# Later preparation, later decoding and a pinned TensorE order in the last plain steps of a fused attention and two-layer kernel

## The chip, the cores and the metric

The kernel runs on one core of one Trainium2 chip. The metric is the device time of one execution in microseconds (us), as the median of several runs.

## The reference, cut to what matters

```python
def reference(**kwargs):
    attn_out = _attn_ref(q, k, v)                     # (4, 8, 576, 64), two sparse masks
    x = attn_out.transpose(0, 2, 1, 3).reshape(2304, 512)
    h = x @ w_in                                      # first layer, 512 -> 2048
    x = (h - tanh(h)) @ w_out                         # 2048 -> 512
    xn = x / sqrt(mean(x * x) + 1e-6) * rms_g         # second layer
    g, val = xn @ w_gate, xn @ w_val                  # 512 -> 1536 each
    return (g / (1 + exp(-g)) * val) @ w_out2         # 1536 -> 512
```

2304 tokens run through attention, then through a first layer, then through a second layer with a gate and a value matrix.

## The kernel before

**Precision.** Weights arrive as 64-bit floats. Each block of 128 x 512 is loaded (`fetch`, L175), put together from its two 32-bit words (ScalarE `scale`, L184 and L186; VectorE `merge`, L196), and split into a high and a low part (ScalarE `high`, L203; VectorE `low`, L207). A product is then three matmuls: high by high, high by low, low by high. All matmuls go through `mm` at L150, so tiles tell them apart.

**The second layer has two forms.** The first 256 tokens go through twelve plain steps (`for f in range(FB)`, L1388). A step f does the gate and the value product of block f (`pe_gv`, 24 matmuls `ps_h<-xn,w`), the activation chain on ScalarE and VectorE (L949 to L953), and two steps later the output product of block f (`pe_o(0, f)`, 6 matmuls `ps_x<-w,p`). The other 2048 tokens go through a scheme with seven products in place of eight (`Stage`, NJ = 2 token blocks by NP = 6 pairs of weight blocks). Its products are numbered and run as 1, then 5 and 2 in the first stage, then 6, 3, 7 and 4 (`both(m, ...)`); each has a gate and a value half of 6 matmuls, `ps_pr<-xt,wt` or `ps_pr<-xt,wo` or `ps_q<-xt,wt`. The output product of plain step 11 is issued in the first stage, behind product 1 (`second()`).

**What the stages need ready.** Two helpers run beside the plain steps:

- `pg`, the generator `preps()`. While the last group of the first layer runs, it normalises the tokens; 39 of its pieces are taken there. Seven are left when the plain steps begin: `conv(m)` for m = 1, 2, 5, 6, 3, 7, 4. Each makes the token operand `xt[m]` of product m: for 5, 6, 7 and 4 a difference (VectorE, L1039), then for each a high part (ScalarE, L1058) and a low part (VectorE, L1059), all of 128 x 1024.
- `decode`, which makes weight operands for the stages on POOL. For each pair and for gate and value it has four items: load the plain weights back from memory (`load`, SP DMA `wa<-v`, L291), sums (`sums`, 4 POOL instructions, L302), and two halves (`half`, each a POOL copy L285 and a POOL subtraction L286 into `wo`). Items 0 to 7 are pair 0: its gate (0 to 3) and its value (4 to 7); the load of both stands in item 0. Product 5 needs `got[2]` (first half of the gate) and `got[3]` (first half of the value); products 3 and 7 need `got[4]` and `got[5]`.

**Order.** A compile-time scheduler orders each engine's instructions by priority, which is program order with some pieces raised (the activation chain by 400, the stage's chain by 300), over a modelled time line. From the end of the first layer the SP queue is in program order (`manual_schedule`), so its DMAs stand as written: at each step the weight loads (`st2.to`), the stores of split weights (`store.to`, L363), then the loads of `decode`; at step 8 first `pairs[0].fetch((0, 1))` (L280). `store.plain` goes out on ScalarE's queue (L344). TensorE is in program order from behind the plain steps (L1403) on; inside the plain steps the scheduler is free, and may also put matmuls of the first stage between those of the last plain steps.

**Rooms.** Split weights, fetched weights and `wo` share 20 slots (`wts`); raw weights have 3 (`rawb`); the loaded `wa`, the sums `ws` and the differences `tr` of `conv` share 4 (`tmp`). Plain steps use PSUM banks by `f % 6`; steps 10 and 11 use `ps_x`.

Of the kernel before, what the change touches and what calls it, by code (L numbers as in the profile page):

```python
# [34 lines left out]
def attn_moe_moe_kernel(  # L35
# [25 lines left out]
    B, _, NC, D = q_str.shape  # L61
    NT, DM = out.shape
    FA = w_in.shape[0]
    FB = w_gate.shape[0]
# [16 lines left out]
    def runs(s):  # L81

        r = []
        for i, (b, t) in enumerate(subs[s]):
            if r and r[-1][0] == b and r[-1][1] + r[-1][2] == t:
                r[-1][2] += 64
            else:
                r.append([b, t, 64, 64 * i])
        return r
# [36 lines left out]
    for s in range(len(subs)):  # L126
        if len(runs(s)) > 1 or s in LANES:
            _, t0, n, _ = runs(s)[0]
# [20 lines left out]
    def mm(out_, lhsT, rhs, start, stop):  # L149
        nc.tensor.matmul(out_, lhsT, rhs, start=start, stop=stop, skip_group_check=True)  # L150
# [179 lines left out]
    decode = Decode()  # L330
# [606 lines left out]
    def pe_gv(j, f):  # L937
        r, n = [], R0
        bank = (bank_h, bank_m, bank_h, bank_m, bank_x, bank_x)[f % 6]("ps_h")
        for k, kd in enumerate(("gate", "val")):  # L940
            ps = bank[:, k * n:k * n + n]
            w, x = w2[kd, f].t, xn[j]
            seq = [(a, e, c) for c in range(4) for a, e in ((0, 0), (0, 1), (1, 0))]
            for i, (a, e, c) in enumerate(seq):
                mm(ps, w[:, a, c, :], x[:, e, c, :], i == 0, i == len(seq) - 1)
            r.append(ps)
        with tc.high_priority(400):
            s = pb.tile([128, n], F32, tag="s", name="s", bufs=3)
            nc.scalar.activation(out=s, in_=r[0], func=ACTF.Silu, scale=WS)  # L949
            nc.vector.scalar_tensor_tensor(out=s, in0=r[1], scalar=WS, in1=s, op0=ALU.mult, op1=ALU.mult)  # L950
            t = pb.tile([128, 2, n], F32R, tag="p", name="p", bufs=3)
            nc.scalar.copy(out=t[:, 0], in_=s)
            nc.vector.tensor_tensor(out=t[:, 1], in0=s, in1=t[:, 0].bitcast(F32), op=ALU.subtract)  # L953
        p_of[j, f] = t

    def pe_o(j, f):
        if f == 0:
            oacc[j] = [ps_x.tile([128, 512], F32, tag="x", name="ps_x") for _ in range(R0 // 128)]
        w, p = w2["out2", f].t.rearrange("p s c f -> p s (c f)"), p_of.pop((j, f))
        for t in range(R0 // 128):  # L960
            for i, (a, e) in enumerate(((0, 0), (1, 0), (0, 1))):
                mm(
                    oacc[j][t], p[:, e, t * 128:t * 128 + 128], w[:, a, :],
                    f == 0 and i == 0, f == FB - 1 and i == 2,
                )
# [337 lines left out]
    for g, f, a, e in units:  # L1303
        if g == 0:
            st1.to(2 * (f + 4))
        elif f == 0:
            if g == 1:
                queue0.close()
                order = ctx.enter_context(ExitStack())
# [8 lines left out]
        if g == NG - 2 and f == 14:  # L1318
# [3 lines left out]
            order = ctx.enter_context(ExitStack())  # L1322
# [65 lines left out]
    for f in range(FB):  # L1388
        if f == FB - 4:
            pairs[0].fetch((0, 1))  # L1390
        st2.to(max(3 * (f + 2), N1 + (len(w2_order) - N1) * (f + 1) // (FB - 2)))
        store.plain(st2.i - 1)
        store.to(st2.i - 6)
        pe_gv(0, f)
        for _ in range(3 if f < FB - 2 else 40):
            next(pg, None)
        decode.to(max(0, min(8, 8 * (f - 4) // 6)))
        if f > 1:
            pe_o(0, f - 2)
    pe_o(0, FB - 2)  # L1400
    store.plain(len(w2_order))
    store.to(len(w2_order))
    ctx.enter_context(tc.manual_schedule(engines={mybir.EngineType.PE, mybir.EngineType.SP}))  # L1403

    def second():
# [149 lines left out]
```

## Time and profile before

| | before |
|---|---|
| median of 3 runs | 888.45 us (885.4 to 888.65) |
| profiled execution, its own time | 887.88 us |
| its span (first to last instruction) | 886.1 us |
| mean granted TensorE clock | 0.992 |
| TensorE (PE) busy | 866.5 us, 98% of the span |
| VectorE (DVE) busy | 629.8 us, 71% |
| ScalarE (ACT) busy | 413.9 us, 47% |
| POOL busy | 250.6 us, 28% |

Busy times are shares of the whole span; stages differ. "Idle before" is time in which the engine stood still just before an instruction, with what released it. A matmul's end is modelled, so the distance between two starts is the better measure of a run of matmuls.

### The profile page before, as it was taken

To read this page: it belongs to the slowest core of one execution; us is meant where nothing else is said; L and a number is where in the kernel's file an instruction comes from. 1 tells how busy PE (TensorE), PEld (TensorE's weight loads), DVE (VectorE), ACT (ScalarE), POOL (GpSimd) and SP (SyncE) were. 2 spreads that over 40 slices of the span, in tenths; PEclk is the share of its full clock that TensorE was granted. 3 is DMA by queue.
4 is the path that set the end of the run, shared out by engine and by line. 5 is a ranking of instruction groups with operands and counts; after the bars stand their busy time and mean duration, and the time that the engine had idled before them with its cause. 6 is when DMAs were issued, how large, how long until landed. Compare 5 with 4: busy or idle time off the path is not lost.

```text
span 886.1 us, 14047 instructions
## 1 busy us (share of the span) xinstructions
PE 866.5 (98%) x5091; PEld 722.7 (82%) x5091; DVE 629.8 (71%) x1290; ACT 413.9 (47%) x916; POOL 250.6 (28%) x309
## 2 busy tenths in 40 slices
PE   7999999999999999999999899999999999999998
PEld 4888888888998887888889877888788888888886
DVE  5999778888779887657778945569688553445544
ACT  6887633333543333878657644533325324322230
POOL 0000147695366853000000679846200000000000
PEclk8999999999999999999999999999999999999999
DMA  9965224311313000889977999765661288544002
GB/s 302 368 223 178 74 75 156 104 57 36 115 55 110 25 19 27 330 306 370 412 252 227 352 372 336 299 230 214 211 216 48 75 320 353 177 149 136 1 1 95
DMA packets 63717, 164.12 MB, mean 185 GB/s; under 512 B 10080, under 2 KB 21728, under 8 KB 63648
## 3 DMA queue, kind: packets, MB, share of 16 engines
q1 hardware_dynamic: 61088, 159.56, 51.1%
q10 hardware_dynamic: 2560, 3.67, 1.2%
q8 instruction: 40, 0.66, 0.3%
q14 instruction: 29, 0.24, 0.1%
HBM read 119.16 MB, written 44.04 MB: 184 GB/s over the span
## 4 chain that ended last, share of the span: by engine, by line
PE 58%; DVE 10%; POOL 7%; issue 2%; ACT 2%; DMA 1%; SPq 0%; ACTq 0%; DVEq 0%; POOLq 0%
PE ps_pr L150 20%; PE ps_o L150 14%; PE ps_h L150 10%; PE ps_x L150 9%; POOL pr L675 5%; DVE so L715 4%; PE ps_q L150 4%; POOL pr L708 1%; DVE tg L860 1%; DVE g L871 1%; DMA wt<-w 1%; DMA w<-w 1%; DVE s L1108 0%; DVE sm L451 0%; POOL ws L302 0%
## 5 line engine op out<-in xcount | busy, mean ns | idle before, releaser
L150 PE MATMUL ps_h<-xs,w 128*128 128x512 f32 (+1 forms) x984 | 214.6, 367 | 0.7 <-DVE tg L860 0.7
L150 PE MATMUL ps_x<-g,w 128*128 128x512 f32 (+1 forms) x984 | 214.2, 366 | 0.0
L150 PEld LDWEIGHTS ps_h<-xs,w 128*128 128x128 f32 x984 | 169.9, 190 | 30.5 <-DVE tg L860 1.3
L150 PEld LDWEIGHTS ps_x<-g,w 128*128 128x128 f32 x984 | 168.5, 189 | 30.4 <-ACT g L866 0.4
L150 PE MATMUL ps_pr<-xt,wt 128*128 128x512 f32 x576 | 137.6, 390 | 2.0 <-DVE s L1118 1.1
L150 PE MATMUL ps_o<-wt,p 128*128 128x512 f32 x576 | 136.0, 389 | 0.0
L150 PEld LDWEIGHTS ps_pr<-xt,wt 128*128 128x128 f32 x576 | 107.7, 188 | 26.2 <-DVE s L1118 2.0
L150 PEld LDWEIGHTS ps_o<-wt,p 128*128 128x128 f32 x576 | 108.1, 188 | 22.5
L675 POOL TENSOR_TENSOR pr<-sk,sq 128x256 f32<-128x256 f32 (+2 forms) x101 | 82.6, 852 | 133.0 <-DMA sq<-in_q_str_dram 107.3
L866 ACT CAST g<-tg 128x512 fp32r<-128x512 f32 (+1 forms) x82 | 46.5, 567 | 101.3 <-DVE tg L860 101.2
L1129 ACT COPY u<-ps_pr 128x512 f32<-128x512 f32 x72 | 41.9, 587 | 103.5 <-PE ps_pr L150 103.4
L708 POOL TENSOR_TENSOR pr<-sv,se 128x288 f32<-128x288 f32 (+12 forms) x104 | 69.7, 691 | 57.0 <-DVE so L715 19.8
L1181 DVE SCALAR_TENSOR_TENSOR osum<-ps_o,osum 128x512 f32<-128x512 f32 x80 | 54.8, 687 | 27.2 <-PE ps_o L150 26.6
L302 POOL TENSOR_TENSOR ws<-wa 128x256 f32<-128x256 f32 x24 | 24.6, 1044 | 170.4 <-DVE w L207 152.2
L715 DVE TENSOR_REDUCE so<-pr 128x16 f32<-128x272 f32 (+11 forms) x104 | 64.9, 653 | 9.0 <-POOL pr L708 8.6
L150 PE MATMUL ps_pr<-xt,wo 128*128 128x512 f32 x288 | 67.4, 389 | 0.0
L150 PEld LDWEIGHTS ps_pr<-xt,wo 128*128 128x128 f32 x288 | 54.1, 188 | 11.3
L871 DVE TENSOR_TENSOR g<-tg,g 128x512 fp32r<-128x512 f32 (+1 forms) x82 | 55.3, 676 | 10.6 <-ACT g L866 9.3
L860 DVE SCALAR_TENSOR_TENSOR tg<-ps_h,tg 128x512 f32<-128x512 f32 (+1 forms) x82 | 50.6, 618 | 15.9 <-ACT tg L855 15.6
L855 ACT ACTIVATE tg<-ps_h 128x512 f32<-128x512 f32 (+1 forms) x82 | 44.2, 540 | 34.8 <-PE ps_h L150 34.7
L196 DVE SCALAR_TENSOR_TENSOR ct<-ca,ct 128x512 uint32<-128x512 uint32 x68 | 48.0, 713 | 16.6 <-ACT ca L186 16.0
L680 DVE TENSOR_REDUCE sc<-pr 128x4 f32<-128x256 f32 (+2 forms) x101 | 43.7, 437 | 12.1 <-POOL pr L675 11.7
(121 smaller groups left out, 1045.7 us busy)
## 6 DMA issues: line engine op xcount, KB each, us to landing
wt<-w SPq DMA_DIRECT2D x84, 512.0 KB, 4.6
w<-w SPq DMA_DIRECT2D x36, 512.0 KB, 6.2
raw<-in_w_out_dram SPq DMA_DIRECT2D x28, 512.0 KB, 5.8
w<-wo SPq DMA_DIRECT2D x24, 512.0 KB, 7.4
raw<-in_w_in_dram SPq DMA_DIRECT2D x16, 512.0 KB, 8.6
raw<-in_w_gate_dram SPq DMA_DIRECT2D x12, 512.0 KB, 6.7
raw<-in_w_val_dram SPq DMA_DIRECT2D x12, 512.0 KB, 7.1
wa<-v SPq DMA_DIRECT2D x24, 256.0 KB, 4.7
```

Source lines behind the costliest of these rows:

```text
L150: nc.tensor.matmul(out_, lhsT, rhs, start=start, stop=stop, skip_group_check=True)
L196: nc.vector.scalar_tensor_tensor(out=t, in0=self.a.bitcast(U32), scalar=3, in1=t, op0=ALU.logical_shift_left, op1=ALU.bitwise_or)
L675: nc.gpsimd.tensor_tensor(out=pr, in0=self.k[:, a:e, :], in1=self.q[:, c - c0:c - c0 + 1, :].to_broadcast([128, e - a, D]), op=ALU.mult,)
L680: pend.append(lambda: nc.vector.tensor_reduce(out=s[:, c - c0, a:e], in_=pr, axis=AX.X, op=ALU.add))
L708: nc.gpsimd.tensor_tensor(out=pr, in0=self.v[:, 0:c + 1, a:e], in1=self.e[:, c - c0, 0:c + 1].unsqueeze(2).to_broadcast([128, c + 1, e - a ...
L715: pend.append(lambda: nc.vector.tensor_reduce(out=o[:, c - g0, a:e], in_=pr.rearrange("l c d -> l d c"), axis=AX.X, op=ALU.add))
L855: nc.scalar.activation(out=t, in_=h_of[g, f, a], func=ACTF.Tanh, scale=WS)
L860: nc.vector.scalar_tensor_tensor(out=t, in0=h_of.pop((g, f, a)), scalar=WS, in1=t, op0=ALU.mult, op1=ALU.subtract)
L866: nc.scalar.copy(out=t[:, 0], in_=t_of[g, f, a])
L871: nc.vector.tensor_tensor(out=t[:, 1], in0=t_of.pop((g, f, a)), in1=t[:, 0].bitcast(F32), op=ALU.subtract)
L1129: nc.scalar.copy(out=u, in_=x[kd])
L1181: nc.vector.scalar_tensor_tensor(out=o, in0=ps, scalar=WS, in1=o, op0=ALU.mult, op1=ALU.add)
```

## The change

Three things change in the loop over the plain steps, and nothing else:

- `pg` is taken later: none before step 5, two pieces at step 5, one at each of steps 6 to 9, the rest at step 10 (before: three at each of steps 0 to 9).
- `decode` is taken later: items up to 2, 4, 6 and 8 at steps 8, 9, 10 and 11 (before: up to 1, 2, 4, 5, 6 and 8 at steps 5 to 10).
- From step 10 to the end of the loop TensorE is in program order: products of step 10, output products of step 8, output products of step 9, products of step 11, output products of step 10. Behind that the order written out before goes on with product 1 of the first stage.

```diff
         store.plain(st2.i - 1)
         store.to(st2.i - 6)
+        if f == FB - 2:
+            order = ctx.enter_context(ExitStack())
+            order.enter_context(tc.manual_schedule(engines={mybir.EngineType.PE}))
+        if f == FB - 1:
+            pe_o(0, f - 2)
         pe_gv(0, f)
-        for _ in range(3 if f < FB - 2 else 40):
+        for _ in range((f >= 5) + (f == 5) if f < FB - 2 else 40):
             next(pg, None)
-        decode.to(max(0, min(8, 8 * (f - 4) // 6)))
-        if f > 1:
+        decode.to(max(0, 8 * (f - 7) // 4))
+        if 1 < f < FB - 1:
             pe_o(0, f - 2)
     pe_o(0, FB - 2)
     store.plain(len(w2_order))
     store.to(len(w2_order))
+    order.close()
     ctx.enter_context(tc.manual_schedule(engines={mybir.EngineType.PE, mybir.EngineType.SP}))
```

## Rows read from the trace of the kernel before

**Rows 1.** Busy time by stretch: plain steps, then the first stage (us, busy, instructions).

```profile
core 0: us, PE busy (x) PEld busy (x) DVE busy (x) ACT busy (x) POOL busy (x), PEclk, DMA share, GB/s
468.00:484.00 16.00, 16.00 (x118) 15.15 (x118) 15.80 (x26) 12.20 (x24) 0.00 (x0) 1.00 0.76 243
484.00:500.00 16.00, 13.45 (x76) 11.58 (x76) 16.00 (x25) 12.77 (x23) 4.57 (x2) 0.89 0.99 326
500.00:521.60 21.60, 20.17 (x123) 17.64 (x122) 14.52 (x18) 9.43 (x20) 16.40 (x15) 1.00 0.99 368
521.60:545.00 23.40, 21.90 (x95) 17.15 (x94) 14.06 (x16) 9.29 (x16) 22.79 (x26) 1.00 1.02 392
```

**Rows 2.** Time line of TensorE: start, us, what, count, idle before and its releaser.

```profile
486.17 0.63 PE L150 MATMUL ps_h<-xn,w 128*128 128x256 f32 x4
487.10 2.25 PE L150 MATMUL ps_h<-xn,w 128*128 128x256 f32 x14 [0.30 <-DVE w L207]
489.70 1.19 PE L150 MATMUL ps_x<-w,p 128*128 128x512 f32 x4 [0.36 <-ACT p L952]
...
493.90 2.26 PE L150 MATMUL ps_h<-xn,w 128*128 128x256 f32 x12 [1.84 <-DVE w L207]
495.96 2.57 PE L150 MATMUL ps_x<-w,p 128*128 128x512 f32 x6
498.37 1.23 PE L150 MATMUL ps_h<-xn,w 128*128 128x256 f32 x9
...
505.89 1.58 PE L150 MATMUL ps_h<-xn,w 128*128 128x256 f32 x12
507.31 1.32 PE L150 MATMUL ps_x<-w,p 128*128 128x512 f32 x5
...
516.95 1.60 PE L150 MATMUL ps_h<-xn,w 128*128 128x256 f32 x12
519.98 1.66 PE L150 MATMUL ps_x<-w,p 128*128 128x512 f32 x6 [1.43 <-ACT p L952]
521.47 2.91 PE L150 MATMUL ps_pr<-xt,wo 128*128 128x512 f32 x12
524.22 2.88 PE L150 MATMUL ps_q<-xt,wt 128*128 128x512 f32 x12
```

**Rows 3.** Groups by line in 458.6 to 521.6, those of `conv` alone.

```profile
L1059 DVE TENSOR_TENSOR xt<-tr,xt 128x1024 fp32r<-128x1024 f32 x4 | 5.3, 1351 | 0.0
...
L1058 ACT CAST xt<-tr 128x1024 fp32r<-128x1024 f32 x4 | 4.1, 1037 | 0.2 <-DVE tr L1039 0.2
L1059 DVE TENSOR_TENSOR xt<-x,xt 128x1024 fp32r<-128x1024 f32 x3 | 3.6, 1218 | 0.0
...
L1058 ACT CAST xt<-x 128x1024 fp32r<-128x1024 f32 x3 | 2.9, 1045 | 0.0
...
L1039 DVE TENSOR_TENSOR tr<-x 128x1024 f32<-128x1024 f32 x2 | 2.4, 1218 | 0.0
L1039 DVE TENSOR_TENSOR tr<-x,tr 128x1024 f32<-128x1024 f32 x2 | 2.4, 1218 | 0.0
```

**Rows 4.** Time line of VectorE, as in rows 2.

```profile
490.57 2.35 DVE L1059 TENSOR_TENSOR xt<-tr,xt 128x1024 fp32r<-128x1024 f32 x2
...
493.17 0.68 DVE L207 TENSOR_TENSOR w<-ct,w 128x512 fp32r<-128x512 f32 x1
...
516.02 1.02 DVE L207 TENSOR_TENSOR w<-ct,w 128x512 fp32r<-128x512 f32 x1 [0.69 <-ACT w L203]
```

**Rows 5.** Time line of the SP queue's DMA issues.

```profile
490.31 2.94 SPq L291 DMA_DIRECT2D wa<-v x4
...
503.62 0.79 SPq L280 DMA_DIRECT2D wt<-w x2
505.48 0.33 SPq L175 DMA_DIRECT2D raw<-in_w_val_dram x1
...
506.38 11.20 SPq L363 DMA_DIRECT2D w<-w x6
```

**Rows 6.** Time line of POOL, first and last of the 16 instructions for pair 0.

```profile
495.43 4.71 POOL L302 TENSOR_TENSOR ws<-wa 128x256 f32<-128x256 f32 x2 [152.24 <-DVE w L207]
...
513.48 3.00 POOL L286 TENSOR_TENSOR wo<-ws,wo 128x512 fp32r<-128x512 f32 x2
```

## The prediction

> **What bounds the kernel now.** I read first the busy times by stretch. TensorE is the bound nearly everywhere, so only a stretch in which it stands still or runs slowly can give time back. Such a stretch lies in the second half of the plain steps: TensorE is busy 16.00 of 16 us in 468 to 484, but 13.45 of 16 in 484 to 500, at a mean granted clock of 0.89, and 20.17 of 21.6 after that [rows 1]. The same rows name the neighbour to suspect: VectorE is busy 15.80 and then 16.00 of 16 us, so from 468 to 500 it has no room.
>
> Next comes TensorE's time line of that stretch [rows 2]. The reader is to see four stops: 0.30 and 1.84 us for VectorE's L207, the low part of a weight; 0.36 and 1.43 us for L952, the activation chain. They sum to 3.93 us. Behind the stop of 1.84 us the next two runs are slow: 12 gate or value matmuls and 6 output matmuls take from 493.90 to 498.37, 4.47 us.
>
> What the stretch would take without stops follows from the same rows. Twelve gate or value matmuls go from 505.89 to 507.31, 1.42 us, 0.118 each. Twelve matmuls of 512 columns go from 521.47 to 524.22, 2.75 us, 0.229 each. So the slow pair should take 1.42 + 6 x 0.229 = 2.79 and loses 1.7 us to the clock. From 486.17 on TensorE still has 2 matmuls of step 6 and 24 for each of steps 7 to 11 (122), the output products of steps 4 to 11 (48), and product 1 (12), and then comes product 5 at 521.47. That is 122 x 0.118 + 60 x 0.229 = 28.1 us; it took 521.47 - 486.17 = 35.3. **At most 7.2 us** can be won here: 3.9 of stops, 1.7 of clock, the rest in the ends and starts of the cut runs.
>
> Last, who is late. VectorE's time line has two low parts of `conv` (2.35 us) at 490.57, and only then, at 493.17, the low part for which TensorE waits until 493.90 [rows 4]. So work that is not needed before the first stage stands ahead of work that is needed at once.
>
> **The change, part by part.**
>
> *`conv` later.* Seven ScalarE copies (4.1 + 2.9 = 7.0 us), seven VectorE low parts (5.3 + 3.6 = 8.9) and four differences (2.4 + 2.4 = 4.8) lose their priority over the weights of the steps before theirs [rows 3]. No work is removed. On VectorE 13.7 us stop being ahead of the weights; pieces for products 1, 2, 5 and 6 (four low parts, two differences, at 1.22 us each 7.3 us) come back at steps 5 to 7, and the scheduler may still use them as fillers. The last weight, the value of step 11, can therefore come forward by between 13.7 - 7.3 = 6.4 us and 13.7 us. The moved copies don't press on TensorE: ScalarE is busy 9.43 of 21.6 us where they go [rows 1]. If this cover fails, product 5 waits for its own `xt`, 1 to 3 us.
>
> *TensorE in order.* The last weight's low part ends at 516.02 + 1.02 = 517.04 [rows 4], and the last run of step 11 starts at 516.95, the two clocks being that close [rows 2]. Before, product 1 had already been slipped in ahead of it (12 matmuls, 2.75 us); after it stood only the run itself, a stop of 1.43 and the last output product, and product 5 began 4.4 us behind the low part. In the new order the low part at time T is followed by its run (1.42), the output product of step 10 (1.37), product 1 (2.75) and the output product of step 11 (1.37): product 5 begins at T + 6.9. The stop of 1.43 is covered, since 4.1 us of other products stand between the last products of step 11 and their output product. But if T did not move, the order alone would cost 6.9 - 4.4 = 2.5 us. Full pace needs T at 521.5 - 7.2 - 6.9 = 507.4, 9.6 us earlier than now. With T earlier by 6.4 to 13.7, product 5 begins between 517.5 and the full-pace 514.3: **4.0 to 7.2 us** won. I take T at 509, near the low end plus a little, as transfers also stand in the way: the DMA engines are already at a share of 0.99 from 484 on [rows 1], and the load of that weight, issued at 505.48, is 10.5 us ahead of its low part [rows 5, 4]. That gives product 5 at 516, some 5.5 us won.
>
> *`decode` later.* Sixteen POOL instructions and four DMA loads move from step 5 to step 8 and on. In the SP queue the loads (490.31 now) go behind the stores and raw loads of steps 6 and 7, the fetch of two weights (503.62), the last raw load (505.48) and two of the six stores from 506.38 on [rows 5]. In today's times that is about 508. But that queue waits for the same weights, and comes forward with them by the same 6.4 to 13.7 us: the loads go out at 495 to 502. From issue to the first POOL work is now 5.1 us (490.31 to 495.43), and the sixteen take 21.05 us (to 516.48) [rows 5, 6]. The operand for the value half of product 5 is ready when three of four halves are done: in the new order, both sums and three halves, some 17 us by today's durations. So it is there between 495 + 5 + 17 = 517 and 524; the value half of product 5 wants it at 516 + 1.4 = 517.4, and had it at 522.8 before. With the middle of that range 3 us would go, at the early end nothing. POOL ran slowly because VectorE was full beside it; the first two sums took 4.71 us, while whole stages of decoding fit in later stretches. I take a wait of 1 us.
>
> A VectorE instruction with two inputs in SBUF and a POOL instruction that reads SBUF exclude each other for their whole length, says the Trainium skill in SBUF — State Buffer, section Who interferes with whom. The trace agrees: the one differing low part of `conv` that ran beside POOL took 4 x 1351 - 3 x 1218 = 1750 ns against 1218 [rows 3]. By that rule the five last `conv` pieces, moved into POOL's hours, would cost 5 x 0.53 = 2.7 us on VectorE, and as much on POOL.
>
> *Sum.* 5.5 won at product 5, 1 given back: **4.5 us**. Nothing behind gives it back unless the second pair's decoding is late; POOL is full in the first stage (22.79 of 23.4 us [rows 1]), but its loads leave the SP queue earlier too. The profiled execution took 887.88 us, 1.78 more than its span, and lies 0.6 under the median; the median less 4.5 is **883.9 us**.
>
> **The rivals.**
>
> *The weights are held by something else* (chance 0.30). If transfers or the 20 slots, not VectorE, set the pace, the last weight comes forward by only 2 to 6 us. For it: the DMA share of 0.99. Against it: VectorE's full rows and the named waits for L207. Product 5 then begins at 518 to 522: 3.5 us faster to 0.5 slower, 885 to 889.
>
> *Decoding late: slower* (chance 0.15). If the SP queue reaches step 8 no earlier than now, the loads go out at 508, the operand is ready at 508 + 5 + 17 = 530, and the value half of product 5 begins at 530 in place of 522.8: 7 us slower, 895.6. The point from which it decides: each us by which the queue comes forward takes one off, so under 7 us forward it is slower than before. VectorE and POOL holding each other up is the same rival's second source: with its 2.7 us on each side the point moves to some 10 us. For it: POOL's slow first sums, the new place behind ten more DMAs. Against it: the queue waits for the very weights that are freed.
>
> *All of it* (chance 0.07): no stop from step 7 on, decoding in time, and some of the 1.5 us that TensorE stands in the first stage [rows 1] gone too: 7 to 8.5 us, 880 to 881.5.
>
> **How the numbers follow.** The forecast case (4.5, from 3 to 6.5 us won, 882 to 885.5) has 0.48. The range reaches to the other cases: down to 880.5, since all of it can't give more than 8.5, and up to 891.5, which holds the held-weights rival and the nearer half of the late decoding. 0.5%, about what a measurement of this kernel tells from no change, is 4.4 us: under 884.0 or over 892.9. Faster takes 0.39 of the forecast case and the 0.07; same the rest of it, the held weights and a little of the late decoding; slower what is left of that: 0.46, 0.41, 0.13.
>
> **What the profile after would show.** Right: no stop for L207 before step 10, a granted clock of 1.0 in 484 to 500, `conv` on VectorE behind the low parts of steps 8 and 9, no stop for L952 ahead of the last output product, product 5 near 517, everything later earlier by the same amount. Wrong: a stop for L207 ahead of the value products of step 11 (the order has taken the filler away), or for POOL's L286 in front of the value half of product 5, or SP issuing `wa<-v` after 503. It would also be wrong if the scheduler, given new priorities, changed the order of steps 0 to 9 in a way that these rows don't show.

## The result, and the profile after

The changed kernel takes **891.52 us** (median; 888.81 to 894.37) against 886.8 us for the kernel before in the same runs (884.77 to 888.65): a ratio of **1.0054**, 95% interval 1.0037 to 1.007. It is 4.7 us slower; 883.9 was forecast, and 891.5 was the upper end of the range.

The profiled execution of the changed kernel has a span of 887.0 us and began its plain steps 2.7 us sooner than that of before, for reasons ahead of the plain steps that no run here traces. (At 888.81 us it is also the fastest of the ten runs, so its loss is not the median's.) So places are compared from an **anchor** that both have just ahead of the plain steps: the start of the last `ps_r` matmul of the normalisation. It lies at 466.27 us in the kernel before and here in the one after (TensorE's time line):

```profile
463.61 0.39 PE L150 MATMUL ps_r<-s,ones 128*128 128x512 f32 x1
```

From the anchor, product 5 begins at 55.20 before (521.47 - 466.27 [rows 2]) and at 55.86 after (519.47 - 463.61), product 2 at 57.95 and 62.07, and the span ends at 419.83 and 423.39. So **0.7 us are lost up to product 5, 3.5 within it**, and 3.6 of these 4.1 are still there at the end.

Busy time by stretch of the kernel after, as in [rows 1]:

```profile
core 0: us, PE busy (x) PEld busy (x) DVE busy (x) ACT busy (x) POOL busy (x), PEclk, DMA share, GB/s
...
484.00:500.00 16.00, 15.23 (x106) 14.00 (x105) 15.21 (x27) 12.58 (x25) 0.00 (x0) 1.00 1.01 387
500.00:521.60 21.60, 17.47 (x83) 13.52 (x81) 9.84 (x13) 8.40 (x16) 11.16 (x12) 0.92 1.03 378
521.60:545.00 23.40, 19.93 (x83) 15.38 (x84) 12.35 (x14) 7.73 (x14) 23.17 (x26) 1.00 0.83 305
```

The stretch from 484 is the gain that was forecast: 15.23 us busy against 13.45, 106 matmuls against 76, the clock at 1.00 against 0.89. (For the earlier start each stretch holds work that lies 2.7 us further on than in [rows 1].) The next gives it back: 83 matmuls against 123. VectorE is idle for more than half of that row, and the DMA engines are full.

TensorE's time line of the kernel after:

```profile
488.71 1.66 PE L150 MATMUL ps_x<-w,p 128*128 128x512 f32 x6 [0.77 <-DVE p L953]
...
504.53 1.52 PE L150 MATMUL ps_pr<-xt,wt 128*128 128x512 f32 x6
...
506.70 1.46 PE L150 MATMUL ps_h<-xn,w 128*128 128x256 f32 x10 [0.22 <-DVE w L207]
508.00 1.55 PE L150 MATMUL ps_pr<-xt,wt 128*128 128x512 f32 x6
511.26 0.50 PE L150 MATMUL ps_h<-xn,w 128*128 128x256 f32 x2 [1.71 <-ACT w L203]
512.43 2.50 PE L150 MATMUL ps_h<-xn,w 128*128 128x256 f32 x10 [0.67 <-DVE w L207]
514.72 2.02 PE L150 MATMUL ps_x<-w,p 128*128 128x512 f32 x6
517.65 1.98 PE L150 MATMUL ps_x<-w,p 128*128 128x512 f32 x6 [0.90 <-ACT p L952]
519.47 1.55 PE L150 MATMUL ps_pr<-xt,wo 128*128 128x512 f32 x6
522.87 0.74 PE L150 MATMUL ps_pr<-xt,wo 128*128 128x512 f32 x2 [1.86 <-POOL wo L285]
524.65 1.19 PE L150 MATMUL ps_pr<-xt,wo 128*128 128x512 f32 x4 [1.04 <-POOL wo L286]
525.68 2.89 PE L150 MATMUL ps_q<-xt,wt 128*128 128x512 f32 x12
```

Between the stop of 0.77 us and 506 nothing stops: the stops of 0.30 and 1.84 us for L207 in [rows 2] are gone. Then step 11 waits for its two weights (0.22; 1.71 and 0.67), runs slowly behind that wait (10 matmuls in 2.50 us against 1.46 for the ten at 506.70; the granted clock of 512.43 to 514.72 is 0.50, the lower of its two levels), and product 5 stands twice for POOL, ahead of its value half (1.86) and within it (1.04).

What the two stops of product 5 come from shows in the time lines of the SP queue and of POOL:

```profile
494.63 1.99 SPq L280 DMA_DIRECT2D wt<-w  x2
499.28 0.33 SPq L175 DMA_DIRECT2D raw<-in_w_val_dram  x1
...
502.21 3.31 SPq L291 DMA_DIRECT2D wa<-v  x4
```

```profile
510.29 1.53 POOL L302 TENSOR_TENSOR ws<-wa 128x256 f32<-128x256 f32 x2 [169.71 <-DMA wa<-v]
...
523.34 1.26 POOL L286 TENSOR_TENSOR wo<-ws,wo 128x512 fp32r<-128x512 f32 x1
```

The loads of decoding go out at 38.6 us from the anchor (before: 24.0 [rows 5]), POOL starts 8.1 us after them, and the value half's operand is ready at 524.60, 14.3 us after POOL's start. TensorE takes it at 524.65.

### The profile page after: what moved, and what is told of

It reads as the page before. It is cut to its first block, busy times and chain, and to the rows that moved or that the text cites. A ratio compares the mean times of both kernels' runs of the same rounds, so it can differ in the third digit from the quotient of the medians.

```text
span 887.0 us, 14045 instructions
## 1 busy us (share of the span) xinstructions
PE 866.1 (98%) x5091; PEld 721.5 (81%) x5091; DVE 627.2 (71%) x1290; ACT 413.0 (47%) x916; POOL 245.2 (28%) x309
## 4 chain that ended last, share of the span: by engine, by line
PE 56%; DVE 12%; POOL 8%; issue 3%; DMA 2%; ACT 1%; DVEq 0%; ACTq 0%; POOLq 0%; SPq 0%
PE ps_pr L150 19%; PE ps_o L150 13%; PE ps_h L150 10%; PE ps_x L150 9%; POOL pr L675 5%; DVE so L715 4%; PE ps_q L150 3%; POOL pr L708 1%; DVE tg L860 1%; DVE g L871 1%; DMA raw<-in_w_val_dram 1%; DMA w<-w 1%; DVE s L1108 1%; DVE p L1113 1%; DVE osum L1181 0%
## 5 line engine op out<-in xcount | busy, mean ns | idle before, releaser
L150 PEld LDWEIGHTS ps_o<-wt,p 128*128 128x128 f32 x576 | 108.1, 188 | 22.4
L302 POOL TENSOR_TENSOR ws<-wa 128x256 f32<-128x256 f32 x24 | 21.3, 909 | 181.9 <-DMA wa<-v 169.7
```

## The experiments

All kernels compute the whole reference. Distances are from the anchor in each run's own profile, worked out as above; "end" is the span less the anchor, minus 419.83. The ratio is to the kernel before, in runs on the same chip. Each kernel has one profile, so a distance is that of one execution; where the two differ, the ratio decides.

| kernel | ratio, 95% interval | product 5 | product 2 | end |
|---|---|---|---|---|
| before | 1 | 55.20 | 57.95 | 0 |
| after (the change) | 1.0054 [1.0037, 1.0070] | 55.86 | 62.07 | +3.6 |
| conv_late | 1.0077 [1.0053, 1.0101] | 59.84 | 62.57 | +4.3 |
| decode_late | 1.0048 [1.0031, 1.0066] | 55.09 | 62.30 | +4.6 |
| order_only | 0.9994 [0.9975, 1.0013] | 55.16 | 57.90 | -0.5 |
| conv_order | 1.0062 [1.0044, 1.0081] | 60.01 | 62.74 | +4.5 |
| conv_decode | 1.0052 [1.0031, 1.0072] | 55.77 | 61.84 | +3.4 |
| load_at_7 | 1.0004 [0.9987, 1.0021] | 55.68 | 58.41 | 0.0 |
| load_at_6 | 1.0008 [0.9994, 1.0022] | 56.54 | 59.27 | +0.3 |
| load7_plain | 1.0001 [0.9986, 1.0017] | 56.00 | 58.73 | +0.3 |
| load7_conv_early | 0.9993 [0.9975, 1.0012] | 54.59 | 57.32 | -2.0 |
| load7_extra | 1.0028 [1.0010, 1.0047] | 57.55 | 60.28 | +1.5 |
| load7_fetch9 | 1.0033 [1.0015, 1.0051] | 58.01 | 60.73 | +1.3 |
| order_fetch9 | 1.0033 [1.0015, 1.0050] | 57.54 | 60.25 | +1.0 |
| conv_late_load7 | 1.0013 [0.9999, 1.0027] | 56.24 | 58.99 | 0.0 |
| conv_late_tr_wts | 1.0061 [1.0041, 1.0082] | 60.12 | 62.85 | +4.2 |
| load6_conv_early | 0.9998 [0.9979, 1.0016] | 55.94 | 58.68 | +0.3 |

### Each part alone, and two without the third

Later preparation alone (conv_late), on the kernel before:

```diff
-        for _ in range(3 if f < FB - 2 else 40):
+        for _ in range((f >= 5) + (f == 5) if f < FB - 2 else 40):
```

> Only the token preparation is taken later; decoding and TensorE's order as before. Theory D (the loss comes from decoding late): the weights of steps 7 to 10 are no longer late, TensorE's stops for L207 before step 10 go, the operand for product 5 is there in time, and the kernel gains 2 to 5 us (ratio 0.994 to 0.998). Theory W (the last weight is held by its transfer, whatever VectorE does, and the order in the last steps costs): the stops before step 10 go, but TensorE waits by as much longer for the last weight; within 1 us of before.

Later decoding alone (decode_late):

```diff
-        decode.to(max(0, min(8, 8 * (f - 4) // 6)))
+        decode.to(max(0, 8 * (f - 7) // 4))
```

> Only the decoding is taken later; preparation and TensorE's order as before. D: the loads of pair 0 go out at about 508 in place of 490, the value half of product 5 waits for POOL, and the kernel loses 4 to 8 us (ratio 1.004 to 1.009). W: no loss, within 1 us.

The TensorE order alone (order_only): the lines with `order`, `pe_o(0, f - 2)` at the last step, and `1 < f < FB - 1`.

> Only TensorE's order from step 10; preparation and decoding as before. D: within 1 us, since what the order puts behind the last weight (an output product, 1.4 us) it gives back by covering the stop of 1.43 us. W: the last weight is as late as before with less to do ahead of it, 2 to 4 us slower (ratio 1.002 to 1.005).

The change without the later decoding (conv_order):

> The change without the late decoding: preparation later and the order from step 10, decoding as before. D: nothing waits for POOL at product 5 and the kernel is faster than before by 2 to 5 us. W: the stops before the last weight stay (2 to 3 us), 1 to 3 us slower than before.

The change without the order, both paces (conv_decode):

> Preparation and decoding both later, TensorE's order as before. Theory D (the loads of pair 0 stand too late in the SP queue, and POOL is behind them): the value half of product 5 waits for POOL as in the changed kernel, 3 to 6 us slower than before, whatever the order of the last steps. Theory W (the order in the last steps costs): some 2 us less lost than in the changed kernel.

**Measured.** The order is worth nothing, alone (0.9994) or on top of the two paces (1.0052 without it, 1.0054 with it). Each pace loses by itself, and the two together lose no more than one: these are not two prices that add up. Theory D held for decode_late, order_only and conv_decode; that the late preparation loses (conv_late, conv_order) neither theory had forecast.

They also lose in different places. Late decoding alone leaves product 5 where it was (55.09) and breaks it open; TensorE's time line of decode_late:

```profile
521.91 0.62 PE L150 MATMUL ps_pr<-xt,wo 128*128 128x512 f32 x2
523.26 1.98 PE L150 MATMUL ps_pr<-xt,wo 128*128 128x512 f32 x6 [0.73 <-POOL wo L286]
527.52 1.80 PE L150 MATMUL ps_pr<-xt,wo 128*128 128x512 f32 x4 [2.28 <-POOL wo L286]
529.12 3.92 PE L150 MATMUL ps_q<-xt,wt 128*128 128x512 f32 x12
```

Product 2 begins 7.2 us behind product 5 where before it was 2.75 [rows 2]. Late preparation alone keeps product 5 whole (2.73 us to product 2) and starts it 4.6 us late. VectorE's time line of conv_late, the last low parts and what stands between them:

```profile
501.99 1.01 DVE L207 TENSOR_TENSOR w<-ct,w 128x512 fp32r<-128x512 f32 x1 [0.69 <-ACT w L203]
504.94 1.21 DVE L1039 TENSOR_TENSOR tr<-x,tr 128x1024 f32<-128x1024 f32 x1
506.18 1.22 DVE L1039 TENSOR_TENSOR tr<-x 128x1024 f32<-128x1024 f32 x1
507.93 2.35 DVE L1059 TENSOR_TENSOR xt<-tr,xt 128x1024 fp32r<-128x1024 f32 x2
510.20 1.22 DVE L1039 TENSOR_TENSOR tr<-x,tr 128x1024 f32<-128x1024 f32 x1
511.33 1.22 DVE L207 TENSOR_TENSOR w<-ct,w 128x512 fp32r<-128x512 f32 x1
```

Five `conv` instructions stand in front of the low part at 511.33, the very thing that the later pace was to end. TensorE waits for it (its time line in conv_late):

```profile
509.06 0.80 PE L150 MATMUL ps_h<-xn,w 128*128 128x256 f32 x2 [3.16 <-ACT w L203]
512.61 2.50 PE L150 MATMUL ps_h<-xn,w 128*128 128x256 f32 x10 [2.75 <-DVE w L207]
```

### The loads of decoding one step earlier, all else as in the change

```diff
-        decode.to(max(0, 8 * (f - 7) // 4))
+        decode.to(max(f >= 7, 8 * (f - 7) // 4))
```

> The change, with only the first item of the decoding (its four loads) at step 7 in place of step 8, so that they stand ahead of the fetch of two weights, the last raw load and two stores. D: the loads go out some 7 us earlier, product 5 no longer waits for POOL, and 2.5 to 4 us of the loss come back (ratio 0.999 to 1.002). Rival V (what holds product 5 is the last weight, late because ScalarE stands in front of its own store's issue): POOL's wait goes but a wait for the last weight takes its place, at most 1 us comes back.

With `f >= 6` in its place (load_at_6):

> The same with the loads at step 6, ahead of the raw load of step 11's gate weight too. D: no more than with step 7, since POOL was in time there already; less, if the two loaded tiles take the room of the differences of the preparation, which then come later, between the last weights (theory R, by which the preparation alone lost 6 us): 1.003 to 1.006.

**Measured.** Four DMA loads moved up by one step give all of the loss back: 1.0004 against 1.0054, product 2 at 58.41 against 62.07. In load_at_7 they go out at 496.00, 30.7 us from the anchor, and product 5 has no stop (SP queue, then TensorE):

```profile
496.00 4.11 SPq L291 DMA_DIRECT2D wa<-v  x4
```

```profile
507.66 0.50 PE L150 MATMUL ps_h<-xn,w 128*128 128x256 f32 x2 [1.28 <-ACT w L203]
509.81 1.64 PE L150 MATMUL ps_h<-xn,w 128*128 128x256 f32 x10 [1.64 <-DVE w L207]
511.24 4.34 PE L150 MATMUL ps_pr<-xt,wt 128*128 128x512 f32 x12
...
520.97 2.89 PE L150 MATMUL ps_pr<-xt,wo 128*128 128x512 f32 x12
523.70 2.88 PE L150 MATMUL ps_q<-xt,wt 128*128 128x512 f32 x12
```

A second step earlier adds nothing. So the loss of the change is the decoding's place behind the SP queue. But the 4 to 5 us that were to be won don't appear: the lead that TensorE has at 505 is gone at product 5. Here it goes at the gate weight of step 11, for which TensorE waits twice (1.28 and 1.64 us; on VectorE a late difference, 1.75 us from 506.87, stands in front of its low part), and in product 1 behind it, which runs at a mean granted clock of 0.63 (4.18 us to 515.42, where 2.75 is full pace).

### Where the lead goes: VectorE, ScalarE's stores, transfers

Three kernels on top of load_at_7. Preparation paced as before (load7_conv_early):

```diff
-        for _ in range((f >= 5) + (f == 5) if f < FB - 2 else 40):
+        for _ in range(3 if f < FB - 2 else 40):
```

> Loads of pair 0 at step 7, the rest of the decoding late, the order from step 10, but the preparation as before. Theory D with VectorE as the bound of the weights (the prediction): the stops for L207 at steps 7 and 8 come back, 2 to 4 us slower than the same with the preparation late (ratio to before 1.002 to 1.005). Theory T (the transfers set the last two weights, so what the earlier steps gain is lost in front of them): no difference to the same with the preparation late, 0.999 to 1.002.

The stores on ScalarE's queue later (load7_plain):

```diff
-        store.plain(st2.i - 1)
+        store.plain(min(st2.i - 1, 3 * (FB - 1)))
```

> The loads at step 7, and the stores of the plain weights of step 11 (gate and value, on ScalarE's queue) issued behind the loop's last step in place of step 8 and 9. V: ScalarE no longer stands 2 to 3 us ahead of the last weight's first pass, its low part is that much earlier, and the kernel ends 1 to 3 us below the same without this. D alone: no difference to the loads at step 7.

Two useless copies of 512 KB from memory to memory in the SP queue at step 7 (load7_extra):

```diff
+        if f == 7:
+            for k in range(2):
+                spare = dram.tile([128, 1024], F32, name=f"spare{k}")
+                nc.sync.dma_start(out=spare, in_=pairs[0].store[k])
```

> Loads at step 7, preparation late, the order from step 10, and two useless copies of 512 KB each from memory to memory ahead of the raw load of step 11's gate weight. T: that load lands later by what the copies take (2.6 us at 400 GB/s, up to twice that if reading and writing count apart), and product 5 by 2 to 5 us. VectorE as the bound: no difference.

**Measured.** With the decoding's loads in place, the pace of the preparation makes no difference that stands clear of the noise: 0.9993 with the old one, 1.0004 with the new. (One profile of load7_conv_early ends 2 us early, which its timed runs don't bear out.) With the old pace the loss of steps 7 and 8 comes back (13.47 us busy and a clock of 0.89 in 484 to 500), but from 500 to product 5 TensorE then has one stop, of 0.31 us; and the last low part ends at 49.55 from the anchor, against 48.97 in load_at_7. So taking `conv` out of the way of the low parts, on which the forecast rested, moves the stops to a later place and wins nothing at the end. The later stores change nothing either (1.0001); but in load_at_7 no store of ScalarE's holds the last weight (its scaling begins 0.02 us after its load has landed), so this says nothing of what such a stop costs in the change. The copies do make a difference: the load of the last weight goes out 2.6 us later, product 5 comes 1.9 us later and the ratio rises to 1.0028. TensorE then waits for the last value, its time line in load7_extra:

```profile
516.46 1.46 PE L150 MATMUL ps_h<-xn,w 128*128 128x256 f32 x10 [0.54 <-DVE w L207]
```

Most of the added transfer shows in the time: 1.05 MB at the 0.396 MB per us that load7_extra moves from 484 to 500 are about 2.6 us (an estimate), and 1.9 arrive. So transfers of these steps lie on the path to product 5; that fewer of them would bring it forward wasn't tried. Whether it is the bytes that count or the two further DMAs as such (hardware, below) this run doesn't tell.

### The fetch of product 1's weights one step later

```diff
-        if f == FB - 4:
+        if f == FB - 3:
             pairs[0].fetch((0, 1))
```

On load_at_7 (load7_fetch9):

> Loads at step 7, preparation late, the order from step 10, and the fetch of two weights for product 1 at step 9 in place of 8, behind the last raw load. T: the last raw load goes out 2 to 3 us earlier and lands earlier; product 5 begins 1 to 3 us earlier, unless product 1 now waits for its weights. VectorE as the bound: no difference.

On the order alone (order_fetch9):

> Only the order from step 10 and the fetch at step 9; preparation and decoding as before. T: the last raw load no longer stands behind the fetch (which waited 6.6 us), the last weight comes 2 to 5 us earlier, and the kernel is 1 to 4 us faster than before (ratio 0.996 to 0.999). VectorE as the bound: no difference to the order alone (0.9994).

**Measured.** Both are slower, by 0.3%. The load did go out earlier, in order_fetch9 at 33.09 from the anchor against 38.35 in order_only, and landed at 42.09 against 45.30. But the last low part ends at 50.72 in both: ScalarE now takes up the gate weight, landed at 507.86, only at 510.24, behind an activation that waits for TensorE, and the value weight after that. So an earlier load alone doesn't bring the last weight forward either. TensorE's time line of order_fetch9 shows what made it slower:

```profile
517.81 1.46 PE L150 MATMUL ps_h<-xn,w 128*128 128x256 f32 x10 [0.53 <-DVE w L207]
519.11 1.55 PE L150 MATMUL ps_x<-w,p 128*128 128x512 f32 x6
520.50 2.88 PE L150 MATMUL ps_pr<-xt,wt 128*128 128x512 f32 x12
523.22 1.52 PE L150 MATMUL ps_x<-w,p 128*128 128x512 f32 x6
524.58 2.88 PE L150 MATMUL ps_pr<-xt,wo 128*128 128x512 f32 x12
```

Product 1 has lost its place ahead of the last value and stands behind it, and product 5 begins 6.8 us after the value's run could start. That is the order that the prediction had assumed for the change itself. In the change, and in order_only, product 1 (`ps_pr<-xt,wt`) still lies in two pieces among the products of step 11, ahead of its value.

### Why the late preparation alone loses: the room of the loads, or the transfers

The differences of `conv` (`tr`) and the loads of decoding (`wa`) share four tiles. Late preparation, with decoding held until step 7 (conv_late_load7), on conv_late:

```diff
-        decode.to(max(0, min(8, 8 * (f - 4) // 6)))
+        decode.to(min(8, 8 * (f - 4) // 6) if f >= 7 else 0)
```

> Late preparation as in the run with that alone, no late decoding of the rest, but the decoding's first piece (the loads of wo) is held until step 7. Theory R (room: the loads of wo, issued at step 5 of the kernel before, sit in two of the four tiles that the differences of xt also need, so the differences come behind the low parts of values 9 to 11 on VectorE): with the loads later the differences are early again, the 4 to 7 us of loss are gone, ratio 0.998 to 1.002, the first matmul of product 5 about 55.5 us behind the anchor. Theory T (transfers: the late preparation loses because of what the DMA queues carry then): no help from this, ratio 1.004 to 1.009, product 5 at 59 to 60.

The differences in the weights' room (conv_late_tr_wts), on conv_late:

```diff
-                out = tmp[0].tile([128, 2, 512], F32, tag="w", name="tr")[:, :, :HT]
+                out = wts.tile([128, 2, 512], F32, tag="w", name="tr")[:, :, :HT]
```

> Late preparation alone, loads of wo at their old place, and the differences of xt put into the weights' room instead of the one that they share with the loads. Theory R: helps as far as the weights' room is free at that time; it is short there too (the weights of steps 9 to 11 stand in it), so I expect little, 1.003 to 1.009, and more than half of the loss gone only if the differences start ahead of the low part of value 10. Theory T: 1.004 to 1.009.

**Measured.** Loads later take most of the loss away (1.0013 against 1.0077; product 5 at 56.24 against 59.84), and the differences are early again, in VectorE's time line of conv_late_load7:

```profile
477.33 1.22 DVE L1039 TENSOR_TENSOR tr<-x 128x1024 f32<-128x1024 f32 x1
...
491.49 1.22 DVE L1039 TENSOR_TENSOR tr<-x,tr 128x1024 f32<-128x1024 f32 x1
...
505.90 1.60 DVE L1039 TENSOR_TENSOR tr<-x 128x1024 f32<-128x1024 f32 x1
```

Three of the four (the one left out is at 482.21) are done by 493; in conv_late three of the four came after 504. Transfers were not the cause there: in conv_late the DMA engines have room in the stretch that loses, and TensorE's clock falls with its stops:

```profile
500.00:521.60 21.60, 15.69 (x74) 13.29 (x74) 17.37 (x19) 11.18 (x19) 15.82 (x14) 0.76 0.78 306
```

The other room was no help (1.0061), and its differences came later still, from 498.98 to 519.45, which is what a room that is full too would do; both theories had allowed such a ratio, so this run doesn't choose between them. So it is shown that early loads of decoding push late differences behind the weights. That it is the shared tiles that do it fits each row, and the records of the traces point there: of all differences in the 17 traces only two carry a wait for POOL, the one at 504.94 in conv_late and one at 503.95 in conv_order, the two kernels with late preparation and early loads that keep the shared room. A difference reads nothing that POOL writes, so what it can wait for is a tile that POOL had before. No run with a free room for the differences alone has been made.

### The best version left

The change with the loads at step 6 and the preparation paced as before (load6_conv_early):

> The change, with the loads of wo at step 6 and the preparation of xt paced as before: the version that should lose nothing of the kernel before and keep the order. The decoding's theory: product 2 starts within 1.3 us of the kernel before (57 to 59 behind the anchor), ratio 0.996 to 1.002. If the order of the output products costs by itself it shows here as 1.002 to 1.004.

**Measured.** 0.9998: nothing lost, nothing won. No version beat the kernel before by more than the noise.

## Why the prediction was wrong

**"The last weight can come forward by between 6.4 us and 13.7 us": the step that failed.** I had worked it out from VectorE's freed time alone. The end of the last low part moved from 50.77 to 48.77 from the anchor (517.04 - 466.27 [rows 4]; after, the low part at 511.24 takes 1.14 us): **2.0 us**. I had also let the SP queue come forward with the weights, because it "waits for the same weights". Ahead of that weight's load it does not. The waits of the SP queue (us in total, times, longest), first before in 500 to 506, then after in 496 to 500:

```profile
SPq L280 <- DMA v<-ct: 6.6, 1, 6.6
SPq L175 <- DMA v<-ct: 1.0, 1, 1.0
```

```profile
SPq L175 <- DMA v<-ct: 2.6, 1, 2.6
SPq L175 <- ACT w L203: 0.4, 1, 0.4
```

`v<-ct` is a store of a plain weight that ScalarE issues: what the fetch and this load wait for is that an older transfer lands. After, that store went out at 492.57 and landed at 499.22, and the load went out at 499.28. (The last line is the issue's own 0.33 us: L203 ran until 499.61, when the load was already out.)

So the load led by 3.5 us (35.67 from the anchor against 39.21 [rows 5]). In load_at_7, with the four loads of decoding ahead of it again, it goes out at 37.95: by these two profiles 2.3 of the 3.5 us are the place that these loads had given up. In the change it landed 3.9 us earlier than before (42.63 against 46.50), but ScalarE then stood at the issue of a store of its own and began the scaling only 2.3 us after the landing (hardware, below). In none of the kernels does the last low part end more than some 2.2 us ahead of that of before (48.54, in conv_decode). This was the rival "the weights are held by something else", with 2 to 6 us forward. load7_conv_early says that it isn't VectorE's work on `conv`, load7_extra that added transfers delay it, and order_fetch9 that behind an earlier load the next holder stands ready, ScalarE's order. Which of them would have to go together to win the 6.4 us stays open.

**"Product 5 begins at T + 6.9": the number right, the reason wrong.** 519.47 - 512.38 = 7.1. But product 1 stood ahead of the last value, as before, and so was no part of it; in its place stood the run (2.29 us at a granted clock of 0.50), two output products (2.02 and 1.82 us), the first of them slow at its start, and a stop of 0.90 for L952. That the sum came out is luck. order_fetch9, where product 1 does stand behind the last value, gives 6.8 by the assumed sum. By that sum an unmoved last weight would cost 2.5 us, and in order_fetch9 product 5 does come 2.3 us later; in the change the order costs nothing, because it doesn't take the filler away.

**"I take a wait of 1 us" for the late decoding: it was the rival that happened.** Its rule, 7 us less what the queue comes forward, holds: by the clock of before the loads would be at 466.27 + 38.6 = 504.9, which is 3.1 ahead of 508, so 3.9 us slower; product 2 came 4.1 later. I had let the queue come forward with the last weight by 6.4 to 13.7, so both wrong terms are one error. Within it, 8.1 us to POOL's start and 14.3 of POOL, 22.4 together, stood where I had 5.1 and 17, 22.1: two misses of some 3 us that cancel by luck. load_at_7 proves the place: the same POOL work, one step earlier in the queue, and the loss is gone.

**POOL and VectorE.** Only two of the five pieces ran in POOL's hours, 0.5 us longer each: the difference at 512.29 took 1.75 us against 1.22 at 476.55, the low part at 515.15 took 1.67 against 1.22. POOL's first two sums, in reverse, took 1.53 us, of which VectorE was busy for 0.85, against 4.71 beside a VectorE that was busy throughout [rows 6]. The rule of the Trainium skill (SBUF — State Buffer, section Who interferes with whom), that such instructions exclude each other, agrees with both. VectorE had time to spare there. POOL had not: two sums at 515.71 took 2.38 us beside VectorE's work, and two at 524.55, with VectorE idle, 1.43. TensorE waits for POOL in product 5, so some of this is part of the loss; how much wasn't tried.

**What was right.** No stop for L207 before step 10, the clock at 1.00 in 484 to 500, `conv` out of the way of steps 8 and 9: all as forecast. The first piece of product 1, with two matmuls more of step 11 still to do, began at 40.9 from the anchor (504.53) against 45.4 (511.64 in the trace of before): some 4.2 us of lead, near the 5.5 that I had expected. It was gone 15 us later. The signs of being wrong came too: the stops for L207 ahead of the value products of step 11 (0.67) and for POOL's L286 (1.04), and, by the clock of before, `wa<-v` after 503 (504.9).

## What to carry to other kernels

Work taken off a full engine moves the stage that follows only as far as the next resource allows: ask of the last item in the chain (here one weight) what released its load (the queue's own waits tell: here an older transfer, not a weight), and how full the queues are, before counting the freed time as lead. A load that is postponed "until it is needed" has to be priced from its place in the queue, with the landing time of full queues and all the work behind it, and the price that decides is the one without the hoped-for lead. Where two paces share a few tiles, test them alone and together: here each lost about as much alone as both.

## What the runs showed of the hardware

**A DMA issue waits for an older DMA, of either queue, and ScalarE with it.** In decode_late ScalarE did nothing for 5 us around one store that it issues itself; its time line:

```profile
507.78 0.39 ACT L949 ACTIVATE s<-ps_h 128x256 f32<-128x256 f32 x1
512.78 0.33 ACTq L344 DMA_DIRECT2D v<-ct  x1
513.14 0.40 ACT L952 CAST p<-s 128x256 fp32r<-128x256 f32 x1 [4.98 <-DMA w<-w]
```

What is behind the issue (the activation chain, the next weight) waits with it. In the kernel after the same store, at 508.16, holds the scaling of the last weight until 508.53, though its load, 6.96 us from 499.28, had landed at 506.24. What the issue waits for the profile names only as a DMA of `w`, but the records of the traces tell more. This program's DMAs, of the SP queue and of ScalarE's together, signal their landing on eight semaphores (counters that an engine can wait for), and in the 17 traces none of 6768 DMAs goes out before the one before it on its semaphore has landed. The store at 508.16 goes out 0.02 us after the landing (508.14) of a store that the SP queue had issued at 500.24, the one at 512.78 in decode_late 0.02 us after that (512.76) of one issued at 505.91. So no more than eight DMAs of this program are under way at once, and with landings 7 us away a late one holds up the other queue too.

What the stop cost the change is not shown. It took 2.3 us of the last weight's lead, but TensorE then stood for POOL until 524.65 in any case. In load_at_7 the issue goes out at 507.00 and holds nothing, but there the load goes out 2.3 us later, so that its last low part is no earlier (48.97 against 48.77).

**A load in full queues lands late.** The loads of decoding took 5.1 us from issue to POOL's start at a DMA share of 0.99 [rows 5, 6, 1], 8.1 at 1.03 after, and 7.7 in decode_late (507.21 to 514.95); a share that is full either way doesn't tell these apart. The queues moved 387 GB/s in 484 to 500. The Trainium skill (DMA: Bandwidth & Descriptors, section Where 436 GB/s comes from) puts the ceiling of the ports at 435 GB/s and that of memory near 358 per core, half of what a stack gives to two cores. This kernel runs on one core, and 387 lies between the two figures; as a limit of one core alone the second does not hold here.
